# Convolution products on VectorE instead of GpSimd, with the products of two neighbouring channels side by side in SBUF

## The chip, the core and the metric

The kernel runs on one core of a Trainium2 chip. A core has a TensorE (PE in the profile; PEld is its weight load), a VectorE (DVE), a ScalarE (ACT), a GpSimd (POOL) and a SyncE (SP), which here only issues DMA transfers. Each engine takes its instructions in the order in which the program gives them. The metric is the device time of one launch in microseconds; it is the median of several runs.

## The reference

Four layers work in turn on x (2048 tokens, 1024 channels): a convolution layer, an MLP, and both once more with the same weights. Each is added to its input.

```python
def _A_ref(q, k, v, shift_k, ssm_k, ssm_D):     # q = layernorm(x)
    k_shift = sum of k_pad[:, t:t + S] * shift_k[:, 3 - t]   # 4 taps, causal
    kv = k_shift * v
    y = causal convolution of kv with ssm_k along the tokens, per channel, by FFT
    y = y + kv * ssm_D
    return q * y

def _B_ref(x, w1, b1, w2, b2):                   # x = layernorm(x); F = 3584
    h = einsum("bsd,df->bsf", x, w1) + b1
    h = relu(h) ** 2
    return einsum("bsf,fd->bsd", h, w2) + b2
```

(The two lines on the taps and on the convolution are put in words.) The convolution's result y does not depend on x, so it is the same in both convolution layers and can be computed while other things run.

## The kernel before

**The MLP.** The work is done in seven units of 512 tokens, `ORDER = [(0,0), (1,0), (0,1), (0,2), (1,1), (0,3), (1,2)]` as (layer, block of tokens). A unit consists of steps, and a step is a group of 12 matmuls of 128 x 512 on TensorE. Every fp32 product is made of three matmuls of split operands (`mm3`, L350 to L354). The splitting is work beside the matmuls: ScalarE rounds a weight tile to its high half (`w_hi`, L1080), VectorE, in places POOL, subtracts that to get the low half (`w_lo`, L1088, tile `whl`), and the same is done with the activations (`relu2`, L1562 and L1565, tile `rl`). Some split weights are stored once and loaded later as finished pairs (`whl<-wd_m`, L1076, issued by SP). L1685 adds matmul results from PSUM to `acc`.

**The convolution.** The sequence is cut in blocks of 256 tokens, and each block is transformed to 128 complex frequencies on TensorE. For the token blocks `sb` = 1 to 3 this runs beside the MLP, in pieces that are threaded into its steps:

- `fwd_x` transforms k·v. VectorE applies the taps (L382) and multiplies by v (L384, tile `fx`), TensorE transposes that (L437) and transforms it, VectorE combines the results (L419 to L424), and SP stores them. `fwd_g` does the like for the long filter (L480 to L501, tiles `fk` and `fg`).
- `prod_stream` (L538 on) multiplies the two in the frequency domain and sums over blocks: for output block j it needs the sum over i of x[i] · g[j − i]. A unit of it has 16 channel groups by 3 products of a three-product complex multiplication, for each `sb`: 48 units, two products each (`jj` = 0, 1), 288 products over all. `load` (L642, SP) brings the operands `cx` and `cg` (two buffers each), `mult` forms all products of one j into `cp` (three buffers), `red` sums them over i into `sm`.
- `fin` then combines the three sums of a group: `fold` (L692), `butterfly` (L696, L697, two instructions). For `sb` > 1 a high and a low half are split off (L571 on ScalarE, L578 on VectorE), the inverse transform runs on TensorE, and the result is stored.

`cp` is a tile of 128 partitions (frequencies) by 128 channel places by j + 1 blocks, with the blocks innermost. `mult` reads both operands with the channels innermost, so its writes lie j + 1 words apart; `red` reads `cp` in order of address. j runs from 2 to 7, so a product has 384 to 1024 elements per partition.

**What sets the order.** `prod_stream` and the transforms are generators. Each step of the MLP lets a generator go on for as much work as `pace` grants. `lag` is a list of work that is due some ticks later, and a product ends with a tick. `lag.at(2, red, ...)` therefore issues the sum two products after its product. After the second product of a unit `fill` asks for the loads of the following units; on SP each load waits until its buffer is free. There is no other scheduler: each engine's queue is what the program writes, in that order. `FIN` names the engine (V or G) of folds and butterflies for each `sb`.

Of the kernel before, what the change touches and what calls it, by code (L numbers as in the profile page):

```python
# [10 lines left out]
F32 = mybir.dt.float32  # L11
F32R = mybir.dt.float32r
AF = mybir.ActivationFunctionType
OP = mybir.AluOpType
AX = mybir.AxisListType
# [4 lines left out]
P = 128  # L20
# [12 lines left out]
CU = 2 * CG  # L33
# [11 lines left out]
NORM_0 = "VA"  # L45
AHEAD_0 = 4
BURST = 1.06
FIN = "GGG"
PACE_SLACK = {1: 74, 3: 10}
PACE_TO = {1: 2}  # L50
PLAIN = 1
# [196 lines left out]
def tile_h3_mlp(ctx: ExitStack, tc: tile.TileContext, q, kT, vT, shk, ssmT, ssmD, w1, b1, w2, b2,  # L248
                fwd_t, pro_t, inv_t, sgn_t, out):
    nc = tc.nc  # L250
    V, A, G, PE, SY = nc.vector, nc.scalar, nc.gpsimd, nc.tensor, nc.sync
# [7 lines left out]
    cv = shut.enter_context(tc.tile_pool(name="cv", bufs=1))  # L259
# [276 lines left out]
    def prod_stream():  # L536
        lag = plag
        sums, inv = [0, 0], [0, 0]  # L538

        def mult(st, xt, gt, j):  # L540
            pr = cv.tile([P, CU, j + 1], F32, name="cp", bufs=3)
            G.tensor_mul(pr.rearrange("p c i -> p i c"), xt[:, 0:j + 1], gt[:, j::-1])  # L542
            st["pr"] = pr

        def red(st, sm, ty, jj):
            V.tensor_reduce(sm[:, ty, jj], st["pr"], axis=AX.X, op=OP.add)  # L546

        def fin(st, sm, sb, g, k):
            s = sm.rearrange("p k j c -> p k (j c)")
            E = ENG[FIN[sb - 1]]  # L550
            if k == 0:
# [81 lines left out]
        def load(n):  # L633
            sb, g, ty = units[n]
            nb = BT * sb + BT
            two = nb <= NBL // 2
            if n % 2 == 0 or not two:
                for nm in ("cx", "cg"):
                    share[nm] = cv.tile([P, 2 if two else 1, nb, CU], F32, name=nm, bufs=2)
            got[n] = [share[nm][:, n % 2 if two else 0] for nm in ("cx", "cg")]  # L640
            for t, src in zip(got[n], (XD[PAIRS[ty][0]], GD[PAIRS[ty][1]])):
                SY.dma_start(t, src[g, :, :nb])  # L642
            when[n] = lag.n

        def fill(n):
            sb = units[n][0]
            room = 3 if BT * sb + BT <= NBL // 2 and n % 2 else 2
            for m in range(n + 1, min(n + room + 1, len(units))):
                if m not in when:
                    if (units[m][0], units[m][1] // 2) not in fwd_done or (m > n + 2 and units[m][0] != sb):  # L650
                        return
                    load(m)

        pair = sm = None
        for n, (sb, g, ty) in enumerate(units):
            while n not in when:
                if (sb, g // 2) in fwd_done:
                    load(n)
                else:
                    lag.tick()  # L660
                    yield None
            while lag.n < when[n] + 2:
                lag.tick()
                yield None
            if ty == 0:
                while sums[0] - sums[1] >= 2:
                    lag.tick()
                    yield None
                sums[0] += 1
                sm = cv.tile([P, 3, BT, CU], F32, name="sm", bufs=2)  # L670
                if g % 2 == 0:
                    pair = {}
            for jj in range(BT):
                j = BT * sb + jj
                st = {"pair": pair}
                mult(st, *got[n], j)
                lag.at(2, red, st, sm, ty, jj)
                if jj == BT - 1:
                    if ty == 2:
                        lag.at(3, fin, st, sm, sb, g, 0)  # L680
                    fill(n)
                lag.tick()
                yield (j + 1) * CU * 1e-3
# [865 lines left out]
    lag = slag  # L1549
    xT = first_block()  # L1550
    pds = prod_stream()
    ml = shut.enter_context(tc.tile_pool(name="ml", bufs=1, reuse_waits="tile"))
    def relu2(st, k):
# [561 lines left out]
    for s, (k, u, c, a, i, tts, w) in enumerate(steps):  # L2115
# [37 lines left out]
        if k == "m1":  # L2153
# [9 lines left out]
            for kk in range(4):  # L2163
                t = slice(kk * P, (kk + 1) * P)
# [8 lines left out]
        elif k == "w2":  # L2173
# [7 lines left out]
            for n in range(2):  # L2181
                t = slice(n * P, (n + 1) * P)
# [11 lines left out]
        else:  # L2194
# [3 lines left out]
            for tt in tts:  # L2198
                t = slice(tt * P, (tt + 1) * P)
# [124 lines left out]
```

## Time and profile before

| | |
|---|---|
| median of 3 runs | 2689.66 us (2689.25 to 2691.11) |
| the profiled execution | 2694.62 us |
| its span | 2692.4 us |
| granted clock | 0.993 |
| convolution products (L542, 288) | 135 to 1750 us |

The span is the time from the profile's first to its last instruction; the profiled execution's own time has a little around it. The page's slices show where the engines work: each digit is a fortieth of the span (67 us), in tenths of busy time.

```profile
PE   7999999899999999999999999999999999999999
DVE  7878888779887878779767765456778787778553
ACT  3444344343434323343233422335444564444342
POOL 2436665156551744417454275000100006646111
```

A row of a group has the line, the engine, the operation, what is written and read, and the count; behind the first bar the busy time and the mean of one in ns; behind the second the engine's idle time just ahead of these instructions, and what ended it. A row of waits reads "engine, tile and line <- what it waited for: total us, times, longest us".

### The profile page before, as it was taken

The numbers are of one execution on the slowest core, as the hardware profiler recorded it, in microseconds if no ns is written. First come the engines' busy times: TensorE is split into PE (matmuls) and PEld (weight loads), VectorE is DVE, ScalarE is ACT, GpSimd is POOL, SyncE is SP. The second block draws the span as 40 slices with busy tenths as digits, with TensorE's granted clock in tenths as the row PEclk, the third lists the DMA queues.
The fourth block names the chain that finished last, engine by engine and source line by source line (L and its number), as shares of the span: only waits on it lengthen the run. The fifth ranks groups of instructions, "written<-read, shape, count | busy, mean of one in ns | idle before, by whom it ended". The sixth has DMA issues, their size and how long they took to land.

```text
span 2692.4 us, 36210 instructions
## 1 busy us (share of the span) xinstructions
PE 2629.6 (98%) x12433; PEld 2204.0 (82%) x12433; DVE 2007.0 (75%) x2957; ACT 1107.6 (41%) x1890; POOL 1010.4 (38%) x641
## 2 busy tenths in 40 slices
PE   7999999899999999999999999999999999999999
PEld 6888787788888888888888888888788778888887
DVE  7878888779887878779767765456778787778553
ACT  3444344343434323343233422335444564444342
POOL 2436665156551744417454275000100006646111
PEclk9999999999999999999999999999999999999999
DMA  7799898679988999888987888689889886888653
GB/s 249 258 306 311 294 306 281 237 267 364 350 299 308 315 328 308 274 293 307 342 304 258 301 291 314 202 266 314 302 295 306 285 300 234 276 259 323 230 188 126
DMA packets 380840, 765.52 MB, mean 284 GB/s; under 512 B 44128, under 2 KB 159472, under 8 KB 377584
## 3 DMA queue, kind: packets, MB, share of 16 engines
q1 hardware_dynamic: 380656, 763.20, 82.7%
q8 instruction: 98, 1.61, 0.2%
q14 instruction: 86, 0.70, 0.1%
HBM read 585.85 MB, written 177.21 MB: 283 GB/s over the span
## 4 chain that ended last, share of the span: by engine, by line
PE 76%; DVE 8%; DMA 8%; POOL 2%; issue 2%; ACT 2%; SPq 1%; DVEq 0%; POOLq 0%; ACTq 0%
PE p L353 22%; PE p L352 22%; PE p L354 22%; PE pt L353 2%; PE pt L354 2%; PE pt L352 2%; PE p L1162 2%; DMA wr<-w 2%; DMA whl<-wd_m 1%; DVE whl L1088 1%; DMA cx<-xd 1%; DMA cg<-gd 1%; DVE st L713 1%; DMA yt<-yd 1%; POOL cp L542 1%
## 5 line engine op out<-in xcount | busy, mean ns | idle before, releaser
L542 POOL TENSOR_TENSOR cp<-cx,cg 128x384 f32<-128x384 f32 (+5 forms) x288 | 543.3, 1899 | 571.4 <-DVE sm L546 378.1
L352 PE MATMUL p<-xh,whl 128*128 128x512 f32 (+1 forms) x1504 | 577.7, 384 | 5.5 <-DMA whl<-wd_m 3.2
L354 PE MATMUL p<-xh,whl 128*128 128x512 f32 (+1 forms) x1504 | 573.5, 381 | 0.6 <-POOL whl L1088 0.6
L353 PE MATMUL p<-xl,whl 128*128 128x512 f32 (+1 forms) x1504 | 573.4, 381 | 0.1
L1080 ACT CAST whl<-wr 128x512 fp32r<-128x512 f32 x545 | 331.7, 619 | 477.1 <-PE p L354 270.6
L1088 DVE TENSOR_TENSOR whl<-wr,whl 128x512 fp32r<-128x512 f32 x495 | 427.5, 875 | 130.7 <-ACT whl L1080 130.1
L352 PE MATMUL p<-whl,rh 128*128 128x512 f32 x1204 | 476.0, 395 | 4.9 <-DMA whl<-wd_m 2.6
L353 PE MATMUL p<-whl,rh 128*128 128x512 f32 x1204 | 471.2, 391 | 4.8 <-DVE whl L1088 4.7
L354 PE MATMUL p<-whl,rl 128*128 128x512 f32 x1204 | 470.6, 391 | 0.0
L352 PEld LDWEIGHTS p<-xh,whl 128*128 128x128 f32 x1504 | 284.1, 189 | 60.9 <-issue 2.4
L354 PEld LDWEIGHTS p<-xh,whl 128*128 128x128 f32 x1504 | 283.6, 189 | 55.5 <-POOL whl L1088 0.8
L353 PEld LDWEIGHTS p<-xl,whl 128*128 128x128 f32 x1504 | 283.9, 189 | 52.4 <-DVE xl L1475 0.3
L1565 DVE TENSOR_TENSOR rl<-wr,rh 128x512 fp32r<-128x512 f32 x140 | 142.4, 1017 | 181.5 <-ACT rh L1562 181.1
L352 PEld LDWEIGHTS p<-whl,rh 128*128 128x128 f32 x1204 | 227.3, 189 | 53.8 <-DMA whl<-wd_m 5.2
L353 PEld LDWEIGHTS p<-whl,rh 128*128 128x128 f32 x1204 | 227.3, 189 | 51.5 <-DVE whl L1088 6.4
L354 PEld LDWEIGHTS p<-whl,rl 128*128 128x128 f32 x1204 | 227.1, 189 | 47.7
L546 DVE TENSOR_REDUCE sm<-cp 128x128 f32<-128x384 f32 (+5 forms) x288 | 249.5, 874 | 11.7 <-POOL cp L542 11.7
L1557 ACT ACTIVATE wr<-p,b1t 128x512 f32<-128x512 f32 x138 | 95.2, 690 | 369.8 <-PE p L354 367.2
L1088 POOL TENSOR_TENSOR whl<-wr,whl 128x512 fp32r<-128x512 f32 x50 | 71.5, 1431 | 274.1 <-ACT whl L1080 257.2
L1685 DVE TENSOR_TENSOR acc<-p,acc 128x512 f32<-128x512 f32 x152 | 99.8, 686 | 83.6 <-PE p L354 83.6
L1044 POOL TENSOR_TENSOR sr<-sr 128x512 f32<-128x512 f32 x14 | 19.9, 1420 | 341.3 <-DMA pd<-wr 303.8
L692 POOL TENSOR_TENSOR sm<-sm 128x512 f32<-128x512 f32 x48 | 69.1, 1440 | 131.5 <-DVE sm L546 123.8
(369 smaller groups left out, 4367.0 us busy)
## 6 DMA issues: line engine op xcount, KB each, us to landing
whl<-wd_m SPq DMA_DIRECT2D x323, 512.0 KB, 5.7
wr<-w SPq DMA_DIRECT2D x441, 256.0 KB, 5.6
wd_m<-whl SPq DMA_DIRECT2D x70, 512.0 KB, 6.4
wr<-td SPq DMA_DIRECT2D x112, 256.0 KB, 4.8
cx<-xd SPq DMA_DIRECT2D x48, 512.0 KB, 5.7
cg<-gd SPq DMA_DIRECT2D x48, 512.0 KB, 6.7
tq<-hd SPq DMA_DIRECT2D x24, 1024.0 KB, 7.4
gd<-fg SPq DMA_DIRECT2D x72, 256.0 KB, 5.9
```

Of the source, the lines that this page charges most:

```text
L352: PE.matmul(o, lh, rh, start=start, stop=False)
L353: PE.matmul(o, lh, rl, start=False, stop=False)
L354: PE.matmul(o, ll, rh, start=False, stop=stop)
L542: G.tensor_mul(pr.rearrange("p c i -> p i c"), xt[:, 0:j + 1], gt[:, j::-1])
L546: V.tensor_reduce(sm[:, ty, jj], st["pr"], axis=AX.X, op=OP.add)
L692: E.tensor_add(s[:, 1:3], s[:, 1:3], s[:, 0:1].to_broadcast([P, 2, s.shape[2]]))
L1080: A.copy(t[:, 0], raws[n]["t"])
L1088: ENG[e[n % len(e)]].tensor_sub(t[:, 1], raws[n]["t"], t[:, 0].bitcast(F32))
L1162: PE.matmul(o, lh, r, start=start, stop=stop)
L1557: A.activation(r, st["o"], AF.Relu, bias=b1t[:, st["f"]:st["f"] + 1])
L1565: V.tensor_sub(st["lo"], st["r"]["t"], st["hi"].bitcast(F32))
L1685: V.tensor_add(accs[tt][:, d], o, accs[tt][:, d])
```

## The change

The products go from POOL to VectorE, and `cp` gets another layout: the channels are taken in pairs, and for a pair and a block the two products lie side by side. `mult` now writes runs of two words, with 2(j + 1) words from run to run; `red` reads every second word. The sum is issued one tick after its product, not two. `FIN` puts folds and butterflies of all three `sb` on VectorE. The arithmetic is the same. From `red` on the line numbers grow by 2.

```diff
-FIN = "GGG"
+FIN = "VVV"
...
         def mult(st, xt, gt, j):
-            pr = cv.tile([P, CU, j + 1], F32, name="cp", bufs=3)
-            G.tensor_mul(pr.rearrange("p c i -> p i c"), xt[:, 0:j + 1], gt[:, j::-1])
+            pr = cv.tile([P, CU // 2, j + 1, 2], F32, name="cp", bufs=3)
+            two = [t.rearrange("p i (c v) -> p i c v", v=2) for t in (xt[:, 0:j + 1], gt[:, j::-1])]
+            V.tensor_mul(pr.rearrange("p c i v -> p i c v"), *two)
             st["pr"] = pr

         def red(st, sm, ty, jj):
-            V.tensor_reduce(sm[:, ty, jj], st["pr"], axis=AX.X, op=OP.add)
+            V.tensor_reduce(sm[:, ty, jj].rearrange("p (c v) -> p c v", v=2), st["pr"].rearrange("p c i v -> p c v i"),
+                            axis=AX.X, op=OP.add)
...
                 mult(st, *got[n], j)
-                lag.at(2, red, st, sm, ty, jj)
+                lag.at(1, red, st, sm, ty, jj)
```

On VectorE, around the place that the profile of before has at 282 to 289 us (`sb` = 1, unit 1 of the MLP), the queue was this, with weight splits (L1088), sums (L546) and two instructions of `fwd_g` (L485, L486) among others:

```order
L1088 TENSOR_TENSOR whl<-wr,whl 128x512
L546 TENSOR_REDUCE sm<-cp 128x128 x2
L485 SCALAR_TENSOR_TENSOR pt<-pt,fk 128x512
L486 TENSOR_TENSOR pt<-pt,fk 128x512
L1088 TENSOR_TENSOR whl<-wr,whl 128x512
L546 TENSOR_REDUCE sm<-cp 128x128 x2
L500 TENSOR_TENSOR fg<-pt,fg 128x2x2x64
L501 TENSOR_TENSOR fg<-pt,fg 128x2x2x64
```

The same place after the change:

```order
L1090 TENSOR_TENSOR whl<-wr,whl 128x512
L543 TENSOR_TENSOR cp<-cx,cg 128x3x64x2
L698 TENSOR_TENSOR sm<-sm 128x256
L699 TENSOR_TENSOR sm<-sm 128x4x64
L547 TENSOR_REDUCE sm<-cp 128x128
L543 TENSOR_TENSOR cp<-cx,cg 128x4x64x2
L547 TENSOR_REDUCE sm<-cp 128x128
L485 SCALAR_TENSOR_TENSOR pt<-pt,fk 128x512
L486 TENSOR_TENSOR pt<-pt,fk 128x512
L1090 TENSOR_TENSOR whl<-wr,whl 128x512
L543 TENSOR_TENSOR cp<-cx,cg 128x3x64x2
L547 TENSOR_REDUCE sm<-cp 128x128
```

Between two weight splits there are now products, the butterfly's two halves (L698, L699) and sums, where there were sums alone; a sum has the product that it needs right ahead of it or one instruction group before.

On POOL the queue of the same stretch was products, folds (L692) and butterflies (L696, L697) without anything between them:

```order
L692 TENSOR_TENSOR sm<-sm 128x512
L542 TENSOR_TENSOR cp<-cx,cg 128x3x128
L696 TENSOR_TENSOR sm<-sm 128x256
L697 TENSOR_TENSOR sm<-sm 128x4x64
L542 TENSOR_TENSOR cp<-cx,cg 128x4x128
L542 TENSOR_TENSOR cp<-cx,cg 128x3x128
```

After the change it is what is left for POOL between 135 and 1750 us, weight splits (L1090) and additions to `acc` (L1804):

```order
L1090 TENSOR_TENSOR whl<-wr,whl 128x512 x5
L1804 TENSOR_TENSOR acc<-acc,px 128x1024 x4
L1090 TENSOR_TENSOR whl<-wr,whl 128x512 x7
L1804 TENSOR_TENSOR acc<-acc,px 128x1024 x4
L1090 TENSOR_TENSOR whl<-wr,whl 128x512 x2
L1804 TENSOR_TENSOR acc<-acc,px 128x1024 x12
```

In all, 288 products, 48 folds and 96 butterfly halves have gone from POOL's queue to VectorE's: the listing of POOL has 132 rows where it had 569, that of VectorE 3062 where it had 2583 (a row can stand for several equal instructions). The queues of TensorE, ScalarE and SP hold the same instructions in the same order.

## The prediction

> **What bounds the kernel now.** I read the page's first lines, then the windows, the waits and the groups of the one stretch in which convolution products run, 135 to 1750 us.
>
> ```profile
> PE 2629.6 (98%) x12433; PEld 2204.0 (82%) x12433; DVE 2007.0 (75%) x2957; ACT 1107.6 (41%) x1890; POOL 1010.4 (38%) x641
> 135.00:1750.00 1615.00, 1588.84 (x7627) 1338.64 (x7627) 1246.50 (x1719) 617.81 (x1095) 768.22 (x466) 0.99 0.86 298
> ```
>
> The second row gives, for the stretch, the busy time of PE, PEld, DVE, ACT and POOL. PE sets the end: the change leaves all its matmuls in place, and 1615 − 1588.84 = 26 us of PE idle time is all that the stretch could give back. So the change acts on the time only through what PE waits for:
>
> ```profile
> PE pt L437 <- DVE fx L384: 9.2, 3, 6.7
> PE p L353 <- DVE whl L1088: 4.7, 2, 4.5
> PE p L1771 <- DVE wr L1762: 3.8, 1, 3.8
> PE pt L612 <- DVE fg L501: 2.3, 1, 2.3
> POOL cp L542 <- DVE sm L546: 378.1, 90, 27.1
> ```
>
> (Total, number, longest.) PE waits for VectorE in a few bursts, 9.2 + 4.7 + 3.8 + 2.3 = 20.0 us. The last row says that POOL, which forms the products, mostly waits for a free `cp` buffer: its speed holds nothing up by itself.
>
> VectorE is slower in this stretch than it need be. First the stretch, then 1750 to 1900, where no products run:
>
> ```profile
> L1088 DVE TENSOR_TENSOR whl<-wr,whl 128x512 fp32r<-128x512 f32 x284 | 276.7, 980 | 44.3 <-ACT whl L1080 44.2
> L1565 DVE TENSOR_TENSOR rl<-wr,rh 128x512 fp32r<-128x512 f32 x134 | 138.2, 1032 | 164.5 <-ACT rh L1562 164.2
> L382 DVE SCALAR_TENSOR_TENSOR fx<-fx,shkt 128x512 f32<-128x512 f32 x72 | 82.1, 1141 | 1.8
> L578 DVE TENSOR_TENSOR yl<-sm,yh 128x256 fp32r<-128x256 f32 x64 | 67.1, 1088 | 0.0
> L501 DVE TENSOR_TENSOR fg<-fk 128x256 f32<-128x256 f32 x24 | 19.9, 828 | 0.0
> L1685 DVE TENSOR_TENSOR acc<-p,acc 128x512 f32<-128x512 f32 x140 | 91.8, 686 | 72.2 <-PE p L354 72.2
> ...
> L1088 DVE TENSOR_TENSOR whl<-wr,whl 128x512 fp32r<-128x512 f32 x42 | 28.2, 686 | 8.7 <-ACT whl L1080 8.6
> L1565 DVE TENSOR_TENSOR rl<-wr,rh 128x512 fp32r<-128x512 f32 x6 | 4.2, 693 | 16.9 <-ACT rh L1562 16.9
> L786 DVE SCALAR_TENSOR_TENSOR yt<-px,mv,yt 128x512 f32<-128x512 f32 x8 | 6.0, 746 | 0.0
> L1600 DVE TENSOR_TENSOR cp<-cp 128x256 f32<-128x256 f32 x3 | 1.3, 425 | 0.1
> ```
>
> Instructions with two SBUF inputs are longer by up to 1.6 times while POOL works; L1685, with one input in PSUM, is 686 ns in the stretch and is not.
>
> **Removed.** Products, folds and butterflies leave POOL:
>
> ```profile
> L542 POOL TENSOR_TENSOR cp<-cx,cg 128x384 f32<-128x384 f32 (+5 forms) x288 | 543.3, 1899 | 571.4 <-DVE sm L546 378.1
> L1802 POOL TENSOR_TENSOR acc<-acc,px 128x1024 f32<-128x1024 f32 x20 | 54.5, 2758 | 13.5 <-issue 10.9 <-DMA px<-b 1.5 <-DMA wr<-w 1.0
> L1088 POOL TENSOR_TENSOR whl<-wr,whl 128x512 fp32r<-128x512 f32 x14 | 19.0, 1357 | 93.5 <-ACT whl L1080 91.1 <-DMA wr<-w 2.3
> L692 POOL TENSOR_TENSOR sm<-sm 128x512 f32<-128x512 f32 x48 | 69.1, 1440 | 131.5 <-DVE sm L546 123.8 <-DMA whl<-wd_m 4.3 <-ACT whl L1080 3.4
> ```
>
> L1802 and L1088 stay: 73.5 of POOL's 768 us, a tenth. Relief on VectorE: 284 × (980 − 686) = 83.5; L1565 134 × (1032 − 693) = 45.4; L382 72 × (1141 − 746) = 28.4 (L786 as the free form); L578 64 × (1088 − 425) = 42.4; L501 24 × (828 − 425) = 9.7: 209 us. Smaller groups of the same kind I put at 20. Nine tenths of 229 is **205 us**.
>
> **Added.** 288 products, 48 folds of 512 elements, 96 butterfly halves of 256. For the products I take VectorE's reduces, which read the same element counts:
>
> ```profile
> L546 DVE TENSOR_REDUCE sm<-cp 128x128 f32<-128x384 f32 (+5 forms) x288 | 249.5, 874 | 11.7 <-POOL cp L542 11.7
> L546 DVE TENSOR_REDUCE sm<-cp 128x128 f32<-128x1024 f32 x48 | 57.9, 1207 | 0.0
> L546 DVE TENSOR_REDUCE sm<-cp 128x128 f32<-128x512 f32 x48 | 32.4, 675 | 1.2 <-POOL cp L542 1.2
> L546 DVE TENSOR_REDUCE sm<-cp 128x128 f32<-128x384 f32 x48 | 26.1, 543 | 10.5 <-POOL cp L542 10.5
> ```
>
> At 512 elements a reduce takes 675 ns, a two-input instruction 686, so products cost 249.5 × 686 / 675 = 254 us. Folds and butterflies: 48 × (0.686 + 2 × 0.425) = 74. Two corrections come from the starts of neighbours (start, duration):
>
> ```profile
> 284.40 0.69 DVE L485 SCALAR_TENSOR_TENSOR pt<-pt,fk 128x512 f32<-128x512 f32 x1
> 285.00 0.69 DVE L486 TENSOR_TENSOR pt<-pt,fk 128x512 f32<-128x512 f32 x1
> ...
> 630.11 0.16 DVE L727 RECIPROCAL rs<-sd 128x4 f32<-128x4 f32 x1
> 630.30 0.16 DVE L735 TENSOR_TENSOR rt<-rs 128x4 f32<-128x4 f32 x1
> ```
>
> An instruction starts about 0.08 us before its predecessor ends: 432 × 0.08 = −35. If it needs the predecessor's result it starts about 0.035 after the end instead. The reduce now comes one tick after its product, and in the new order 180 of 288 reduces stand right behind their own product: 180 × 0.115 = +21. Added: 254 + 74 − 35 + 21 = 314; net of the relief **+109 us** of VectorE's time, 1246 to about 1355 of 1615 (84%), and 2007 to about 2116 in all.
>
> **The layout** is the unknown. Products are written in runs of two words, and the reduce now reads every second word. No row shows VectorE doing either. The nearest is POOL's: its product of 512 elements wrote single words j + 1 apart in 1519 ns, its contiguous L692 took 1440:
>
> ```profile
> L542 POOL TENSOR_TENSOR cp<-cx,cg 128x512 f32<-128x512 f32 x48 | 72.9, 1519 | 15.3 <-DVE sm L546 15.3
> ```
>
> That is 5%, or 12 us on the reduces, next to nothing. The upper end is half rate: the reduce's slope is (1207 − 543) / 640 = 1.04 ns per element, and 48 × 128 × (3 + 4 + 5 + 6 + 7 + 8) = 202,752 elements give +211 us. A gain has no source, since the reduce already reads in address order. I take **0** and keep 0 to 211.
>
> The Trainium skill speaks against the change here: "Vector Engine (DVE) Microarchitecture Reference", section "5.2 Measured stream behaviour on trn2 (trn3 not measured)", gives full rate only to runs of two adjacent words; one source hopping at every element takes 1.73 instead of 1.054 ns a column. By it the writes are free, while the reduces grow by an estimated 0.68 × 202,752 = 137 us. "SBUF — State Buffer", section "Door 1: The DMA port swizzle (why `[64,N]` ≈ `[32,N]`)", asks only for two accesses to each 16-byte line, which a step of two words still makes; by it the reduce costs nothing extra. The trace shows neither.
>
> **Where PE waits.** The largest stall, seen closely:
>
> ```profile
> 275.20 1.78 DVE L1088 TENSOR_TENSOR whl<-wr,whl 128x512 fp32r<-128x512 f32 x1
> 285.60 1.62 DVE L1088 TENSOR_TENSOR whl<-wr,whl 128x512 fp32r<-128x512 f32 x1
> 293.89 3.67 DVE L382 SCALAR_TENSOR_TENSOR fx<-fx,shkt 128x512 f32<-128x512 f32 x3
> 297.49 1.21 DVE L500 TENSOR_TENSOR fg<-fk 128x256 f32<-128x256 f32 x1
> 298.62 1.49 DVE L501 TENSOR_TENSOR fg<-fk 128x256 f32<-128x256 f32 x1
> 300.03 1.48 DVE L1088 TENSOR_TENSOR whl<-wr,whl 128x512 fp32r<-128x512 f32 x1
> 302.26 1.10 PE L437 MATMUL pt<-ident,fx 128*128 128x128 f32 x4 [6.70 <-DVE fx L384]
> ```
>
> VectorE was busy nearly throughout from 272 on, and PE waited 6.70 us for its L384. These rows get shorter by 2.8 (three L1088, 4.88 − 3 × 0.686), 1.6 (L382 against 3 × 0.746 − 0.16) and 1.85 (L500, L501): 6.3 us. Some 1.8 us in which VectorE waited here for POOL's products go too (part of the 11.7 above). Into the same piece the new order puts ten products (five of 384 and five of 512 elements, 543 and 686 ns), two folds and a butterfly pair: 6.1 + 1.4 + 0.85 − 14 × 0.08 = 7.2, and about eight dependent neighbours, 0.9: 8.1 us against 8.1. The stall stays. The other bursts have the same mixture, and I put all of them at **0 us**.
>
> **The loads.** A product on VectorE also waits for its `cx` and `cg`, and whatever is queued behind it there (weight splits L1088, which PE needs) waits along. SP waits too: its next load needs the buffer that a product releases, and the weight-pair loads L1076, which matmuls need, stand behind it.
>
> ```profile
> POOL cp L542 <- DMA cg<-gd: 182.0, 43, 14.4
> SPq L642 <- POOL cp L542: 59.6, 30, 5.6
> SPq L1076 <- PE p L354: 417.5, 169, 12.4
> ```
>
> POOL reaches a product early and waits for the transfer, 43 times; VectorE comes to it up to three `cp` buffers later, and against the landings seen here all but a few transfers are there first. SP's release comes some 3 us later by the same comparison, while L1076 mostly waits for PE and has room. I put **+2 us** on PE here, bounds 0 and +10.
>
> **Sum.** 2694.6 (profiled execution, span 2692.4) + 0 + 2 = 2696.6. The median of the runs, 2689.66, lies 5 us below the profiled time, so 2691.6: **2692 us**.
>
> **Rivals.**
> - *The relief wins.* If products overlap better than a reduce, or the stalls sit where relief outweighs additions, PE's waits on L384 and L501 vanish: 2692 − 9.2 − 2.3 gives about **2680**; with all 20.0 us gone, 2672. For it: the rows above lose up to 1.1 us each. Against: ten products fit in exactly what they free.
> - *The strided reduce costs* (the slower side). At half the upper price, 0.52 ns per element, the ten reduces of a burst (448 elements on average) take 2.3 us more. With some eight such bursts PE waits 18 us longer, and about 4 go where VectorE is fullest, 2692 + 22 = **2714**; its busy time is then 1355 + 105 = 1460 of 1615. It decides from about 0.15 ns per element, where a burst loses 0.7 us and eight of them what a measurement can tell. At half rate, 37 us in the bursts and 15 where VectorE is full: 2744. By the Trainium skill's 1.73 ns (the section 5.2 above) it would be an estimated 2692 + 29 = 2721.
> - *Loads come late.* VectorE stops at missing `cg`, SP holds L1076 back: the upper bound, +10 in place of +2: **2700**.
> - *The change does not do what it says:* excluded, since the order shows the products on VectorE.
>
> **How the numbers follow.** The forecast 43%, the relief 25%, the strided reduce 20%, late loads 12%. The range is 2678 to 2716: it takes in the relief's likelier point and the strided reduce at half its upper price, and leaves out both far ends. About 0.2%, 5.4 us, is what a measurement of this kernel tells from no change: 2684.3 to 2695.0. Faster 0.26 (the relief, and little of the forecast), same 0.42, slower 0.32 (the two slower rivals).
>
> **What would show it.** The reduces: 543 to 1207 ns as now if the step of two words is free, near 0.7 and 1.7 us if the middle price is right. Products of the same lengths, 0.54 to 1.2 us. L1088 near 700 ns and L578 near 425 in the stretch. VectorE about 2116 us in all. PE's wait for L384 still there, 5 to 7 us. SP's L642 released by VectorE. I am wrong if VectorE's total lies over 2200, or if PE's waits for VectorE differ much from 20 us.

## The result

| | before | after |
|---|---|---|
| median of the runs | 2690.39 us (2689.25 to 2691.49, 4 runs) | 2713.19 us (2707.67 to 2717.08, 4 runs) |
| ratio | | 1.0083 (95% interval 1.0061 to 1.0106) |
| the profiled execution | 2694.62 us, span 2692.4 | 2709.6 us, span 2707.8 |

The change makes the kernel slower by 0.8%. The time lies in the range given, 2678 to 2716, but the forecast of 2692 was 21 us too low. The medians lie 22.8 us apart and the two profiled executions 15.0 us; what follows from the traces can explain only the latter. The busy times of the profile after, and the windows row of the stretch 135 to 1750 us (PE, PEld, DVE, ACT, POOL):

```profile
PE 2634.6 (97%) x12433; PEld 2202.2 (81%) x12433; DVE 2109.7 (78%) x3389; ACT 1106.7 (41%) x1890; POOL 317.3 (12%) x209
135.00:1750.00 1615.00, 1580.01 (x7544) 1325.01 (x7543) 1339.55 (x2136) 613.02 (x1089) 74.84 (x34) 0.99 0.86 296
```

VectorE works 2109.7 us, 103 more than before; PE has 8.8 us less of its work done in the stretch. What PE waited for there, and what SP waited for, from the waits of the same window:

```profile
PE pt L437 <- DVE fx L384: 8.8, 4, 3.9
PE p L352 <- DMA whl<-wd_m: 7.2, 8, 2.2
PE p L353 <- DVE whl L1090: 5.4, 4, 3.3
PE p L352 <- DVE acc L1687: 1.7, 1, 1.7
SPq L644 <- DVE cp L543: 266.4, 82, 11.4
```

Two things are new. PE waits for pair weights (`whl<-wd_m`) 7.2 us instead of 1.6. And SP stands before its loads of `cx` and `cg` (L644) 266 us in place of 59.6, 82 times in place of 30.

The groups of VectorE, 135 to 1770 us:

```profile
L1090 DVE TENSOR_TENSOR whl<-wr,whl 128x512 fp32r<-128x512 f32 x285 | 207.3, 733 | 28.5 <-ACT whl L1082 24.3 <-DMA td<-cp 3.8 <-ACT sd L723 0.3
L543 DVE TENSOR_TENSOR cp<-cx,cg 128x1024 f32<-128x1024 f32 x48 | 60.6, 1262 | 0.0
L547 DVE TENSOR_REDUCE sm<-cp 128x128 f32<-128x1024 f32 x48 | 58.4, 1218 | 1.1
L543 DVE TENSOR_TENSOR cp<-cx,cg 128x384 f32<-128x384 f32 x48 | 26.6, 554 | 0.0
L547 DVE TENSOR_REDUCE sm<-cp 128x128 f32<-128x384 f32 x48 | 26.5, 552 | 1.9
L580 DVE TENSOR_TENSOR yl<-sm,yh 128x256 fp32r<-128x256 f32 x64 | 26.3, 453 | 0.0
```

Splits and `yl` are nearly as short as they are without POOL (980 to 733, 1088 to 453 ns). The sums took 543 to 1207 ns and now take 552 to 1218: reading every second word costs next to nothing.

**Where the time goes.** TensorE runs the same matmuls in the same order in both kernels, so the start of a matmul after, less the start of the same matmul before, says how far the kernel has fallen behind at that place. This is worked out from the two traces, in us; the runs that follow have their columns here too (three buffers: e1, two ticks: e8, less work: e5, load later: e10). In e10 some matmuls stand at other places in the order, so its column is rough.

| time before | after | three buffers | two ticks | less work | load later |
|---|---|---|---|---|---|
| 200 | −1.3 | −1.8 | −2.2 | −0.8 | −1.3 |
| 400 | 0.5 | 4.5 | −6.0 | −10.7 | 9.5 |
| 425 | 7.0 | 9.6 | −3.3 | −10.7 | 15.8 |
| 600 | 6.6 | 7.9 | −4.6 | −15.9 | 11.1 |
| 650 | 11.4 | 8.1 | 0.6 | −18.0 | 12.3 |
| 1225 | 12.4 | 7.8 | 2.3 | −19.6 | 15.7 |
| 1775 | 16.5 | 10.9 | 9.6 | −18.4 | 19.6 |
| 2600 | 15.4 | 10.7 | 9.0 | | 19.1 |

After 1775 us nothing more is lost. The first column has two parts: some 8 us up to 600, most of them between 400 and 425; and 10 us from 600 to 1775, the largest piece of them between 600 and 650. (4 us come after 1225; their cause is open.) The burst that the prediction worked out is not among the places where time is lost. PE's wait at its end, 6.70 us before, is now this one:

```profile
300.59 1.10 PE L437 MATMUL pt<-ident,fx 128*128 128x128 f32 x4 [3.91 <-DVE fx L384]
```

A wait of 1.66 us has come ahead of it, at 292.82 us, and the kernel stands at −0.6 us at 310, after −1.3 at 200. The two largest places look like this. First the end of the burst before 413 us, VectorE and then PE:

```profile
412.73 0.68 DVE L384 TENSOR_TENSOR fx<-fx 128x512 f32<-128x512 f32 x1
413.55 1.10 PE L437 MATMUL pt<-ident,fx 128*128 128x128 f32 x4 [3.83 <-DVE fx L384]
```

PE waits 3.83 us for L384, where before it did not wait. VectorE was busy 24.62 us of the 24.90 from 387.8 to 412.7 us. Before, the same piece, from L419 to L384, lasted from 385.4 to 408.0, 22.6 us: it became 2.3 us longer, and the piece ahead of it (from the L384 before to L419) went from 10.6 to 12.1. Then the second place, SP's queue and PE:

```profile
623.75 0.38 SPq L1098 DMA_DIRECT2D wd_m<-whl  x1
633.18 0.32 SPq L644 DMA_DIRECT2D cx<-xd  x1
633.56 0.42 SPq L644 DMA_DIRECT2D cg<-gd  x1
634.07 0.38 SPq L1078 DMA_DIRECT2D whl<-wd_m  x1
...
640.20 0.47 PE L352 MATMUL p<-xh,whl 128*128 128x512 f32 x1 [2.20 <-DMA whl<-wd_m]
```

SP issues nothing for 9 us, until a product has released the buffer of `cx`. The pair weights behind it go out at 634.07 and PE waits 2.20 us for weights. Before, the same pair load was issued at 621.38:

```profile
615.23 0.32 SPq L1096 DMA_DIRECT2D wd_m<-whl  x1
620.50 0.32 SPq L642 DMA_DIRECT2D cx<-xd  x1
621.38 0.38 SPq L1076 DMA_DIRECT2D whl<-wd_m  x1
```

PE was 6.6 us behind here, so that load is 634.07 − 621.38 − 6.6 = 6.1 us later measured by PE's work.

A wait is not all that PE loses at these places. The windows right behind the two waits, and then the matmuls of the first one in the kernel before (PE's busy time comes first; 0.51, 0.57 and 1.00 are the granted clock):

```profile
413.60:418.90 5.30, 5.30 (x15) 4.34 (x16) 4.86 (x9) 1.10 (x2) 0.00 (x0) 0.51 0.95 306
640.20:644.20 4.00, 4.00 (x11) 3.13 (x12) 3.97 (x6) 0.00 (x0) 0.00 (x0) 0.57 1.07 369
...
409.10:412.00 2.90, 2.90 (x16) 2.48 (x16) 2.90 (x3) 1.49 (x3) 2.80 (x2) 1.00 0.97 334
```

Behind the wait of 3.83 us ten matmuls in a row start 0.43 us apart (414.88 to 418.72); before, the same ten start 0.23 us apart (409.75 to 411.81). So the kernel falls behind by 6.5 us between 400 and 425, not by 3.8. Over the stretch it is the same: PE's busy time falls by 8.8 us, but from 200 to 1775 us the kernel falls behind by 17.8. About half of the loss is not waiting but matmuls that start further apart; at the two places shown, the granted clock is about half of what it was.

### The profile page after: what moved, and what is told of

It is laid out like the page before. It is cut to its first block, busy times and chain, and to the rows that moved or that the text cites. A ratio compares the mean times of both kernels' runs of the same rounds, so it can differ in the third digit from the quotient of the medians.

```text
span 2707.8 us, 36003 instructions
## 1 busy us (share of the span) xinstructions
PE 2634.6 (97%) x12433; PEld 2202.2 (81%) x12433; DVE 2109.7 (78%) x3389; ACT 1106.7 (41%) x1890; POOL 317.3 (12%) x209
## 4 chain that ended last, share of the span: by engine, by line
PE 73%; DVE 12%; DMA 9%; issue 2%; ACT 2%; SPq 1%; POOL 1%; DVEq 0%; ACTq 0%; POOLq 0%
PE p L352 21%; PE p L353 21%; PE p L354 21%; DMA whl<-wd_m 3%; PE pt L352 2%; PE pt L354 2%; PE pt L353 2%; DVE cp L543 1%; DVE whl L1090 1%; DMA wr<-w 1%; PE p L1164 1%; DMA wd_m<-whl 1%; DMA cg<-gd 1%; DVE sm L547 1%; DMA gd<-fg 1%
## 5 line engine op out<-in xcount | busy, mean ns | idle before, releaser
L1090 DVE TENSOR_TENSOR whl<-wr,whl 128x512 fp32r<-128x512 f32 x495 | 356.8, 732 | 114.5 <-ACT whl L1082 107.8
L543 DVE TENSOR_TENSOR cp<-cx,cg 128x384 f32<-128x384 f32 (+5 forms) x288 | 261.4, 908 | 3.1 <-DMA cg<-gd 3.1
L1567 DVE TENSOR_TENSOR rl<-wr,rh 128x512 fp32r<-128x512 f32 x140 | 110.2, 788 | 137.0 <-ACT rh L1564 137.0
L1804 POOL TENSOR_TENSOR acc<-acc,px 128x1024 f32<-128x1024 f32 x20 | 56.0, 2829 | 1002.4 <-DMA wr<-w 347.1
L1090 POOL TENSOR_TENSOR whl<-wr,whl 128x512 fp32r<-128x512 f32 x50 | 72.3, 1446 | 572.6 <-DMA wr<-w 312.6
L354 PE MATMUL p<-whl,tq 128*128 128x512 f32 x276 | 107.4, 389 | 0.0
```

Of the source, the lines that this page charges most:

```text
L354: PE.matmul(o, ll, rh, start=False, stop=stop)
L543: V.tensor_mul(pr.rearrange("p c i v -> p i c v"), *two)
L1090: ENG[e[n % len(e)]].tensor_sub(t[:, 1], raws[n]["t"], t[:, 0].bitcast(F32))
L1567: V.tensor_sub(st["lo"], st["r"]["t"], st["hi"].bitcast(F32))
L1804: G.tensor_add(a, a, st["t"])
```

## The experiments

Two theories: **V**, VectorE's queue is longer in a few full bursts; **L**, SP's loads stand behind products on VectorE, and pair weights come late. Each group of runs shared its runs of the kernel before (median 2690.7 to 2691.9 us), so the ratios compare best.

### Three buffers (e1) and its control (e2)

```diff
-                lag.at(1, red, st, sm, ty, jj)
+                red(st, sm, ty, jj)
```

That is e2. For e1 also, the seven 4 KB buffers of `cp`, `cx` and `cg` being shared out anew. The other tiles that use these buffers are moved to match; that part is left out here:

```diff
-            pr = cv.tile([P, CU // 2, j + 1, 2], F32, name="cp", bufs=3)
+            pr = cv.tile([P, CU // 2, j + 1, 2], F32, name="cp", bufs=1)
...
-                    share[nm] = cv.tile([P, 2 if two else 1, nb, CU], F32, name=nm, bufs=2)
+                    share[nm] = cv.tile([P, 2 if two else 1, nb, CU], F32, name=nm, bufs=3)
```

> The changed kernel with each sum right behind its product, one cp buffer and three buffers each for cx and cg in place of two, so that a load need not wait for the product before last. Theory L (loads: SP stands behind VectorE's products, pair weights arrive late): SP's wait of its loads for products falls from 266 us to under 60 us, PE's waits for pair weights from 12.7 back to about 6 us, and the time falls to 2700 us or below. Theory V (VectorE's queue is longer in bursts): the time stays with the next run's, 2708 to 2717 us, however SP's waits fall.

> The changed kernel with each sum right behind its product (no tick between), two buffers for cx and cg as before: the control for the run with three. The 108 sums that did not stand behind their product now do: 108 x 0.115 = 12 us more of VectorE's time. Theory L: the same as the changed kernel, 2708 to 2717 us, SP's load waits some 266 us. Theory V: up to 3 us more than the changed kernel.

Measured: e1 2707.77 us, ratio 1.0052 (1.0040 to 1.0064); e2 2718.37 us, 1.0096 (1.0083 to 1.0109). The buffers alone are worth 10.6 us. e2 lies 5 us above the changed kernel, a little more than either theory gave, but their intervals overlap. The waits of e2 and then of e1, 135 to 1750 us:

```profile
SPq L644 <- DVE cp L543: 279.7, 84, 15.8
PE p L352 <- DMA whl<-wd_m: 11.7, 9, 4.4
```

```profile
SPq L644 <- DVE cp L543: 13.1, 12, 4.6
PE p L352 <- DMA whl<-wd_m: 1.2, 2, 1.1
PE pt L437 <- DVE fx L384: 9.1, 4, 3.9
```

SP's wait goes, and PE's wait for pair weights with it; in the table above the step between 600 and 650 us shrinks from 4.8 to 0.2. So L holds. It is not all: e1 stays 16 us above the kernel before, where L alone gave 2700 us or less, and its loss up to 600 us is as large as ever.

### One part alone (e3, e4)

```diff
-FIN = "GGG"
+FIN = "VVV"
```

on the kernel before is e3; the reverse on the changed kernel is e4.

> The kernel before with folds and butterflies alone on VectorE; the products stay on POOL. VectorE gets 74 us more, less about a fifth of the relief (157 of POOL's 768 us leave), 40 us. Theory L: no change, 2687 to 2695 us, since no load waits for VectorE. Theory V: 2 to 6 us slower than before.

> The changed kernel with folds and butterflies back on POOL: products alone move. Theory L: all of the loss stays, 2708 to 2717 us. Theory V: VectorE has about 35 us less to do than in the changed kernel (74 less, some 40 of relief given back), so 3 to 8 us of the loss goes, 2703 to 2712 us.

Measured: e3 2700.09 us, 1.0032 (1.0019 to 1.0045); e4 2713.46 us, 1.0075 (1.0062 to 1.0088). Folds alone cost 8.6 us, above what V gave, although no load waits for them: VectorE's time is not free here. But e3 loses nothing in the full bursts up to 600 us (−1.3 there, worked out as in the table above); it falls behind later, to 7.1 us at 1775, where PE waits for VectorE some 6 us longer. Products alone cost all that the whole change costs. That agrees with the figure of L, but it does not set L apart from V: e4's profile has 10.7 us of waits for pair weights, and besides, on VectorE, 8.2 us for L1090, 5.5 for L384 and 4.2 for L501.

### Less work on VectorE (e5)

On e1, so that loads are out of the question. Each product and sum leaves out two of its j + 1 blocks, so this kernel does not compute the convolution:

```diff
-            pr = cv.tile([P, CU // 2, j + 1, 2], F32, name="cp", bufs=1)
+            pr = cv.tile([P, CU // 2, j - 1, 2], F32, name="cp", bufs=1)
-            two = [... for t in (xt[:, 0:j + 1], gt[:, j::-1])]
+            two = [... for t in (xt[:, 0:j - 1], gt[:, j:1:-1])]
```

> The run with three cx and cg buffers, with two of the j + 1 blocks left out of every product and sum: 288 x 256 x 1.04 ns x 2 = 153 us less of VectorE's time, all loads and all instructions kept. Theory V (what is left of the loss there, 2707.8 against 2691.5 us, is that VectorE's queue is longer in a few bursts before 500 us): the bursts lose some 5 us each, PE's steps before 500 us go, and the time falls to 2690 to 2699 us. Against it (the loss comes from waits or positions in the queues, not from the length of the work): it stays at 2703 to 2708 us.

Measured: 2672.84 us, 0.9927 (0.9914 to 0.9940): 35 us below e1. The busy times of e1's page, then of e5's:

```profile
PE 2631.8 (97%) x12433; PEld 2201.4 (81%) x12433; DVE 2117.8 (78%) x3389; ACT 1109.1 (41%) x1890; POOL 316.2 (12%) x209
```

```profile
PE 2623.0 (98%) x12433; PEld 2199.5 (82%) x12433; DVE 1965.9 (74%) x3389; ACT 1106.9 (41%) x1890; POOL 314.9 (12%) x209
```

VectorE works 152 us less. V holds, and more strongly than expected (the time is 17 us below the range that V gave): a microsecond off VectorE was worth 35 / 152 = 0.23 us of the kernel's time. Every loss up to 600 us is gone, and much of what PE waited for before the change as well: PE stands 15.9 us ahead there, and its wait for L384 is 1.2 us where it was 9.2.

### The layout (e6, e7)

e6 has the layout of before on VectorE, e7 has the channels innermost:

```diff
+            pr = cv.tile([P, CU, j + 1], F32, name="cp", bufs=3)              # e6
+            V.tensor_mul(pr.rearrange("p c i -> p i c"), xt[:, 0:j + 1], gt[:, j::-1])
...
+            pr = cv.tile([P, j + 1, CU], F32, name="cp", bufs=3)              # e7
+            V.tensor_mul(pr, xt[:, 0:j + 1], gt[:, j::-1])
```

> The changed kernel with the layout of before: VectorE writes single words j + 1 apart, the sum reads in order of address. If a single word a hop costs what the Trainium skill states in Vector Engine (DVE) Microarchitecture Reference, section 5.2 (1.71 in place of 1.054 ns a column for such a destination, 2.5 for small steps), products take 1.6 to 2.4 times as long, 0.9 to 2.9 us in place of 0.55 to 1.26, VectorE has some 135 to 290 us more to do, and the time is 2730 us or more. If the step costs nothing, products take what they take in pairs and the time stays at 2708 to 2717 us.

> The changed kernel with cp laid out block by block with all 128 channels innermost: products write in order of address, sums read single words 128 words apart. By the rule of the run before, sums take 1.6 to 2.4 times as long as 0.55 to 1.22 us and the time is 2730 us or more; if long steps cost nothing, it stays at 2708 to 2717 us.

Measured: e6 2756.73 us, 1.0237 (1.0220 to 1.0254); e7 2745.77 us, 1.0200 (1.0187 to 1.0213). Groups of e6, then e7:

```profile
L542 DVE TENSOR_TENSOR cp<-cx,cg 128x1024 f32<-128x1024 f32 x48 | 104.9, 2186 | 0.0
L542 DVE TENSOR_TENSOR cp<-cx,cg 128x512 f32<-128x512 f32 x48 | 51.4, 1071 | 0.0
L542 DVE TENSOR_TENSOR cp<-cx,cg 128x384 f32<-128x384 f32 x48 | 32.3, 674 | 1.8 <-DMA cg<-gd 1.8
L546 DVE TENSOR_REDUCE sm<-cp 128x128 f32<-128x1024 f32 x48 | 58.5, 1219 | 1.1
```

```profile
L546 DVE TENSOR_REDUCE sm<-cp 128x128 f32<-128x1024 f32 x48 | 95.7, 1993 | 1.1
L546 DVE TENSOR_REDUCE sm<-cp 128x128 f32<-128x384 f32 x48 | 28.6, 595 | 1.9
L542 DVE TENSOR_TENSOR cp<-cx,cg 128x1024 f32<-128x1024 f32 x48 | 60.4, 1259 | 0.0
```

A product that writes single words 8 words apart takes 2186 ns against 1262 in pairs; 3 words apart it is 674 against 554. A sum that reads words 128 apart takes 1993 against 1218, though with only three blocks 595 against 552. The last row of each is the other half of the comparison, with POOL as idle as in the changed kernel: a sum that reads in order of address takes 1219 (every second word: 1218), a product that writes in order of address 1259 (in pairs: 1262). Neither half of the pair layout costs anything. The pair layout is what makes VectorE fit for the products at all: without it the loss is 54 to 65 us.

### The tick (e8)

```diff
-                lag.at(1, red, st, sm, ty, jj)
+                lag.at(2, red, st, sm, ty, jj)
```

> The changed kernel with the sum two ticks after its product, as before. 180 sums no longer stand behind their own product: 180 x 0.115 = 21 us less of VectorE's time. Theory L (late loads): no change, 2708 to 2717 us, since the product, not the sum, releases cx and cg. Theory V: 2 to 4 us less.

Measured: 2702.95 us, 1.0044 (1.0030 to 1.0058). About half of the change's loss comes from the sum's place, 10 us, which is more than either theory gave. VectorE works 2087.2 us, 22.5 less than in the changed kernel (13.8 of them between 135 and 1750 us). Timeline of the changed kernel, then of e8 (start, duration):

```profile
380.61 0.70 DVE L543 TENSOR_TENSOR cp<-cx,cg 128x512 f32<-128x512 f32 x1
381.35 0.69 DVE L547 TENSOR_REDUCE sm<-cp 128x128 f32<-128x512 f32 x1
381.95 0.68 DVE L1090 TENSOR_TENSOR whl<-wr,whl 128x512 fp32r<-128x512 f32 x1
```

```profile
375.60 0.68 DVE L547 TENSOR_REDUCE sm<-cp 128x128 f32<-128x512 f32 x1
376.19 0.68 DVE L543 TENSOR_TENSOR cp<-cx,cg 128x512 f32<-128x512 f32 x1
376.79 0.55 DVE L547 TENSOR_REDUCE sm<-cp 128x128 f32<-128x384 f32 x1
```

Behind its own product a sum starts 0.04 us after the product's end; otherwise 0.08 us before it. In the changed kernel's trace 172 sums stand right behind a product, so the prediction's 180 × 0.115 = 21 us are there, nearly (172 × 0.115 = 20). What was wrong is their worth: in the table e8 is 4.6 us ahead of the kernel before at 600 us, where the changed kernel is 6.6 behind. From then on e8 loses 14 us, since its loads still wait (SP's L644 266.3 us, PE's pair weights 11.0).

### Both mended, and loads moved (e9, e10)

e9 is e1 with each sum issued ahead of the next product instead of right behind its own, since two ticks need a second `cp` buffer, which would make eight 4 KB buffers in place of seven:

```diff
+                while late:
+                    red(*late.pop())
                 mult(st, *got[n], j)
-                red(st, sm, ty, jj)
+                late.append((st, sm, ty, jj))
```

e10 is e8 with

```diff
-                    fill(n)
+                if jj == 0 and n:
+                    fill(n - 1)
```

> Three buffers each for cx and cg as in the first run, and each sum not right behind its product but ahead of the next one, after whatever VectorE was given between. If the two causes are separate (loads held by products: some 7 us after 600 us; sums right behind their products in full bursts: some 10 us, most of it before 500 us), both gains add: 2707.8 less 5 to 10 gives 2696 to 2703 us, PE's waits for pair weights stay near 1 us, and the PE stream stands at most 4 us behind the kernel before at 500 us. If the run with two ticks gained through the loads, nothing is left to gain here: 2705 to 2709 us.

> The run with two ticks, with each unit's loads issued one product later, so that SP comes to them when the product before is nearer done. Theory L: SP's waits of loads for products fall from about 260 to under 150 us and PE's waits for pair weights from 11 to under 6 us; 2696 to 2701 us against 2703. If the landing is what counts, VectorE waits for cg by more than 20 us (3.9 in the run with two ticks) and the time is 2703 to 2712 us.

Measured: e9 2702.48 us, 1.0043 (1.0030 to 1.0057); e10 2718.72 us, 1.0099 (1.0084 to 1.0113). e9 gains 5 us on e1, but not in the way meant: VectorE still works 2116.9 us, and PE is 6.7 us behind at 600 us. By e9's trace 252 of the 288 sums no longer stand right behind a product. Now 268 products stand right behind a sum, and they start 0.03 us after its end: with a single `cp` buffer a product has to wait until the sum before it has read that buffer. The order was changed, but not the dependence. Whether two ticks and three buffers together would bring back both losses is therefore open; no run has both. e10 shows the other end of L. The waits of e10, 135 to 1750 us:

```profile
SPq L644 <- DVE cp L543: 70.1, 28, 11.0
PE p L352 <- DMA whl<-wd_m: 3.0, 4, 1.6
DVE cp L543 <- DMA cg<-gd: 39.6, 17, 6.0
```

SP and the pair weights wait nearly as little as in the kernel before (59.6 and 1.6), but now VectorE stands 39.6 us before operands that have not landed (3.9 in e8), and all splits behind it with it. The kernel is 16 us slower than e8, and 7 us above what was expected even for late operands.

### The first third only (e11, e12)

Where sb = 2 and 3 stay on POOL:

```diff
         def mult(st, xt, gt, j):
+            if j >= 2 * BT:
+                pr = cv.tile([P, CU, j + 1], F32, name="cp", bufs=3)
+                G.tensor_mul(pr.rearrange("p c i -> p i c"), xt[:, 0:j + 1], gt[:, j::-1])
```

with two ticks, and `FIN` "VGG" (e11) or "GGG" (e12).

> Only the first third of products (sb = 1, before some 500 us) with its folds on VectorE, in pairs and with sums two ticks later; sb = 2 and 3 as before on POOL. The run with two ticks was 3 to 4 us ahead of the kernel before at 550 us and lost all of its time later, where SP's loads waited for products. If stages do not touch each other, that gain is left: 2686 to 2689 us against 2691.5. If the gain of the first stage is lost again at the next hand-over, 2691 to 2694 us.

> Only the products of sb = 1 on VectorE, in pairs and with sums two ticks later; all folds and butterflies, and the products of sb = 2 and 3, on POOL. Compared with the run before, VectorE has 25 us less to do before 500 us (16 folds and 32 butterfly halves) and POOL 52 us more. If VectorE's queue is the bound in the bursts there, 2 to 4 us more is gained: 2684 to 2688 us. If POOL's folds lengthen VectorE's other work by as much as they take from it, 2688 to 2692 us.

Measured: e11 2689.95 us, 0.9993 (0.9983 to 1.0003); e12 2690.09 us, 0.9998 (0.9989 to 1.0007). Neither differs from the kernel before. e11 lies between the two ranges given for it and decides nothing; e12 lies in its second range, where POOL's folds take back what VectorE gains. In e11's profile PE is 3.2 us ahead at 600 us and 2.3 at 1775, but that is within what single executions differ by (2685.4 to 2691.8 us). No run here that computes everything beats the kernel before.

## Why the prediction was right and wrong

- **The bound** was right in that PE sets the end. But a wait was priced at its own length, and the matmuls that start further apart behind it, about half of the loss in the two traces, had no term.
- **The sum of VectorE's time** was right: +109 us foreseen, +103 measured. Products took 261.4 us (254), folds and butterflies 75.6 (74), the relief appeared on the rows named. ("Longer by up to 1.6 times" was misread: the prediction's own rows give 1088 / 425 = 2.6 times for L578 and 1.9 for L501. The sum used the right numbers.)
- **The layout** was right at 0: the reduce's step of two words is free. The rival that priced it gave 2714, close to the measured 2713, for a reason that the groups refute. The range reached up to 2716 because of this rival; without it the slowest time priced was 2700. So it was luck that the measured time lies in the range.
- **The bursts** were wrong. "The other bursts have the same mixture, and I put all of them at 0 us" is the step that failed. The burst that was worked out did come out as foreseen: PE's wait at 300.59 us is 3.91 us, where it was 6.70, and the kernel has lost next to nothing there. In the burst before 413 us, POOL had lengthened less: there the six splits before the change averaged 888 ns (684 after it) and L382 749 (750), and the relief was 1.2 (splits) + 0.9 (L424) + 1.1 (L500, L501) = 3.2 us, plus 1.1 of idle time, against six products, two folds and two butterflies, 6.7 us, less overlap. One burst does not speak for the others. The sign that was named for this, PE's waits for VectorE differing much from 20 us, did not show it either: after the change they add up to 21.6 us. They have moved, and what PE loses behind them is no wait.
- **The tick** was mis-sized by the same step: 21 us were counted on VectorE, but 0.9 us in one burst was set against the relief and the rest at nothing. e8 shows 10 us of the kernel's time.
- **The loads** had the right mechanism and too small a size. "I put +2 us on PE here, bounds 0 and +10": three buffers give 10.6 us (e1 against e2), or some 8 against the changed kernel, by the ratios: at or near the upper bound. Landings seen before the change were compared with VectorE's arrival; SP's own standing still, 266 us where it had been 60, was put at 3 us a release.
- **The rivals**: "loads come late" (2700, 12%) is the one of which the runs confirm a half: SP holds the pair weights back, but VectorE hardly stops at missing `cg` (3.1 us). By itself it would be too little. The loss in the traces is loads and bursts together (the table: 10 us after 600, of which three buffers take 7; 8 before, all of which two ticks take). The two traces end 15 us apart; the other 8 of the measured 22.8 are in no trace, since the profiled execution was 4 us above the median for the kernel before and 4 below it for the changed one.

## What to carry to other kernels

An engine that is 83% busy in a stretch is not free there: adding to VectorE or taking from it moved this kernel by a tenth to a half of a microsecond for each microsecond (e3 8.6 of 88, e5 35 of 152, e8 10 of 22.5), though PE was 98% busy. A wait of the engine that sets the end can cost more than its length: look at the clock right behind it. When a step moves to a busier engine, look at which queue waits for that step's release: here SP issued loads in order, and one load that stood for 9 us before a buffer held back weights that had nothing to do with it. A load issued later only moves the wait to the consumer; another buffer removes it (e1). Before an order is changed to part two instructions, look whether a shared buffer ties them together all the same (e9).

## What the runs showed of the hardware

The lengthening of VectorE's splits, which have two SBUF inputs, comes with single instructions of POOL. In the changed kernel only 16 of the stretch's L1090 and L1567 instructions took over 0.8 us; each of them overlaps with an instruction of POOL, and of all the others only one does. POOL, then VectorE:

```profile
549.25 10.92 POOL L1804 TENSOR_TENSOR acc<-acc,px 128x1024 f32<-128x1024 f32 x4
...
549.86 2.37 DVE L1567 TENSOR_TENSOR rl<-wr,rh 128x512 fp32r<-128x512 f32 x1 [7.27 <-ACT rh L1564]
552.15 2.92 DVE L1090 TENSOR_TENSOR whl<-wr,whl 128x512 fp32r<-128x512 f32 x1
554.99 5.74 DVE L1567 TENSOR_TENSOR rl<-wr,rh 128x512 fp32r<-128x512 f32 x2
```

While POOL adds four times 128x1024 (2.73 us each), VectorE gets through one 0.69 us instruction in each of them. The Trainium skill, "SBUF — State Buffer", section "🔬 SBUF: two separate sides", tells of a shared port pair that is held for a whole instruction; these rows agree.

On strides, for 1024 elements: single words two words apart are read as fast as in order of address (1218 ns against 1219 in e6), words eight apart are written in 2186 ns against 1262 in pairs, words 128 apart read in 1993 against 1218. The Trainium skill, "Vector Engine (DVE) Microarchitecture Reference", section "5.2 Measured stream behaviour on trn2 (trn3 not measured)", asks for runs of two adjacent words, and the pairs written here at full rate agree. For single words 4 KiB apart its 1.71 ns (written) and 1.73 ns (read) against 1.054 are factors of 1.62 and 1.64; the factors here are 1.73 and 1.64. Its 2.50 ns for a written step of 24 words, a factor of 2.37, is not reached at 8. For the step of two words the measurement decides against it.
